# Two-layer feed-forward after gated retention on one core: the first four retention chunks in another order, and six tiles in the first run instead of five

## The chip, the cores and the metric

The kernel runs on one core of one Trainium2 chip. The metric is the device time of one execution, in microseconds (us). The kernel before was timed three times: 582.33, 582.37 and 582.92 us, median 582.37 us.

## The reference, cut to what matters

```python
# attention: retention with one decay per head, q, k, v are (2, 8, 768, 64)
gamma = 1.0 - 2.0 ** (-5.0 - np.arange(H))
scale = 1.0 / np.sqrt(D)
for t in range(S):
    state = gamma * state + einsum('bhd,bhe->bhde', k[:, :, t], v[:, :, t])
    y[:, :, t] = scale * einsum('bhd,bhde->bhe', q[:, :, t], state)
# y becomes x, (1536 tokens, 512); then two layers, w_in (512, 2048), w_out (2048, 512)
x = (mish(x @ w_in)) @ w_out          # h * tanh(log1p(exp(h)))
x = (elu(x @ w_in2)) @ w_out2
```

All of it is float32.

## The kernel before, in words

**Retention.** The 768 steps of each of the two batches are cut into six chunks of 128, twelve chunks in all, numbered so that chunks 0, 2, 4 ... are batch 0 and 1, 3, 5 ... batch 1. Each chunk has a tile `qk` (queries and keys, head dimension across partitions) and a tile `kv` (keys and values, time across partitions), 512 KB each. Chunks 0 to 3 use the functions `scores` (matmuls q·k into `sc`, L227, then the decay mask on VectorE, L234), `scale_k` and `scale_q` (GpSimd products `kd`, L188, and `qd`, L203, `qd` from chunk 2 on) and `attend` (y from state and `qd`, L251, y from v and masked scores, L257, and the new state `st`, L266; then `xh` on ScalarE, L275, `xl` on VectorE, L276, and the state on VectorE, L282 or L286). Chunks 4 to 11 use `scores64` (L309, L316; masks L324 and two states L331) and `attend64` (L353, L360; then copy `t` on ScalarE, L372, y + t on VectorE, L375, `xh`, L377, `xl`, L379). Four chunks make one block of 512 tokens, `x[0]`, `x[1]`, `x[2]`, each as a high and a low part.

**The layers.** The work is a list of tiles (layer, block, feature chunk f). Tile n does `up(n)` (12 matmuls into h: high weight by `xh`, low weight by `xh`, high weight by `xl`, L401), the activation, and three tiles later `down` (12 matmuls, L458). `runs` sets their order: layer 0, block 0, features 0 to FIRST-1; then block 1, features 0 to 7; then block 0, FIRST to 7; and so on. Only `x[0]` must stand before `up(0)`; `x[1]` must stand before tile FIRST. `steps` puts the retention steps of chunks 4 to 11 into the tiles' loop; in tile n they stand behind `up(n)` on TensorE.

**Weights.** They come as packed 64-bit words in 64 halves of 512 KB, `halves`, in the order of first use. Each half goes through `fetch` (DMA into `st`, four buffers, L109), `dec_fields` (two ScalarE activations, L116 and L118), `dec_join` (two VectorE instructions, L127 and L133; then the next `fetch`) and `dec_split` (high part `w0h` or `w1h` on ScalarE, L146, low part on GpSimd, L147). In tile n of the loop, `dec_split` is done for the halves that were joined in tile n-1, behind the retention's steps; at the end of the tile come `dec_join` for the halves whose fields were made in tile n-1, and `dec_fields` for one or two new halves, as `credit` and the due times `need` have it.

**Order.** Instructions are issued in the written order, each engine is a queue. All DMAs are issued by SyncE (SP), also in the written order. Half k of the weights is called half k below, its parts high k and low k.

Of the kernel before, what the change touches and what calls it, by code (L numbers as in the profile page):

```python
# [36 lines left out]
Q = P // 2  # L37
N_MASK, N_TQ, N_TK = H * P, NPAIR * P, CPB * H
N_CT = N_MASK + N_TQ + N_TK
FIRST = 5  # L40


@with_exitstack
def retention_then_two_ffn(
# [134 lines left out]
    def scale_k(c):  # L179
        kv = raw[c][1]  # L180
        i = c // B
        early = c < CPT

        rows = P if i < CPB - 1 else Q
        kd = (gpool if early else qd_p).tile(
            [P, H, D], F32, tag="gl" if early else "kd", name="kd"
        )
        nc.gpsimd.tensor_tensor(  # L188
            out=kd[:rows], in0=kv[:rows, 0], in1=tk[:rows, i].to_broadcast([rows, H, D]),
            op=ALU.mult,  # L190
        )
        scaled[c] = (None, kd)

    def scale_q(c):
        qk = raw[c][0]
        i = c // B
        early = c < CPT
        if i == 0:
            return
        qd = (gpool if early else qd_p).tile(  # L200
            [P, NPAIR, P], F32, tag="gh" if early else "qd", name="qd"
        )
        nc.gpsimd.tensor_tensor(out=qd, in0=qk[:, 0], in1=tabs.get(i, tq), op=ALU.mult)  # L203
        scaled[c] = (qd, scaled[c][1])

    def load_tab(i):
        tabs[i] = qd_p.tile([P, NPAIR, P], F32, tag="tab", name="tab", bufs=2)
# [5 lines left out]
    def scale_chunk(c):  # L213
        scale_k(c)
        scale_q(c)

    def psum(tag, name):
        return (psh if tag == "h" else psa).tile([P, NPAIR, P], F32, tag=tag, name=name)
# [17 lines left out]

        return rest

    def attend(c, tags=("h", "h")):

        kv = raw.pop(c)[1]
        at, (qd, kd) = scored.pop(c), scaled.pop(c)
        i = c // B
        v = kv[:, 1]
        state = states[c % B]
        y = psum(tags[0], "y")


        if i:
            for j in range(NPAIR):  # L250
                nc.tensor.matmul(  # L251
                    y[:, j], state[:, j], qd[:, j],
                    start=j == 0, stop=False, skip_group_check=True,
                )
        for j in range(NPAIR):
            for r in range(2):
                nc.tensor.matmul(  # L257
                    y[r * D:(r + 1) * D, j], v[:, 2 * j + r], at[:, r, j],
                    start=not i, stop=True, skip_group_check=True,
                )  # L260
        if i < CPB - 1:
            st = psum(tags[1], "st")
            for j in range(NPAIR):
                for r in range(2):
                    sl = slice(r * D, (r + 1) * D)
                    nc.tensor.matmul(  # L266
                        st[sl, j, sl], kd[:, 2 * j + r], v[:, 2 * j + r], start=True, stop=True
                    )

        def rest():  # L270
            b, o = divmod(c, CPT)
            if o == 0:
                x[b] = new_x(b)
            xh, xl = (a[:, :, o * P:(o + 1) * P] for a in x[b])
            nc.scalar.copy(out=xh, in_=y)  # L275
            nc.vector.tensor_tensor(out=xl, in0=y, in1=xh.bitcast(F32), op=ALU.subtract)  # L276
            if i < CPB - 1:
                for r in range(2):
                    sl = slice(r * D, (r + 1) * D)
                    if i:  # L280
                        new = compact[c % B] = slots[c % B][0]
                        nc.vector.tensor_tensor(  # L282
                            out=new[sl], in0=st[sl, :, sl], in1=state[sl, :, sl], op=ALU.add
                        )
                    else:
                        nc.vector.tensor_copy(state[sl, :, sl], st[sl, :, sl])  # L286

        return rest

# [200 lines left out]
    with tc.manual_schedule():  # L490
# [9 lines left out]
        for c, tag in ((2, "xh1"), (3, "xl1")):  # L500
# [6 lines left out]
                qk.rearrange("p a (j t) -> p a j t", t=P),  # L507
                kv.rearrange("p a (h d) -> p a h d", d=D),
            )
        for c in (2, 3):  # L510
            nc.sync.dma_start(
                out=raw[c][1].rearrange("p a h d -> p (a h d)"), in_=qkv[c, :, 2 * DM:]
            )
            fetch()
        fetch()
        fetch()
        started = done = 0
        N = len(tiles)
# [8 lines left out]
        def join():  # L527
            nonlocal started
            dec_fields(started)
            dec_join(started)  # L530
            started += 1

        def split_w():
            nonlocal done
            dec_split(done)
            done += 1

        ta, th, tb = ("a0", "a1"), ("h", "h"), ("a2", "a3")
        for i in range(3):
            warm = psa.tile([P, NPAIR, P], F32, tag=f"a{i}", name="warm")  # L540
            nc.tensor.matmul(warm, states[0][:, 0], states[0], start=True, stop=True)
        scale_chunk(0)
        scores(0, ta)()
        scale_chunk(1)
        scores(1, th)()
        scale_chunk(2)
        attend(0, tb)()
        scores(2, ta)()
# [12 lines left out]
        join()  # L561
        dec_fields(started)
        split_w()
        load_chunk(5)
        joined, credit = done, 0.0
        started += 1
# [14 lines left out]
        for n in range(N + LAG):  # L581
            todo = steps.get(n, [])
            rests = []
            if n < N:
                up(n)
                if todo:
                    f, *args = todo[0]
                    rests.append(f(*args))
            full = down(n - LAG) if n >= LAG else []
            for f, *args in todo[1:]:  # L590
                rests.append(f(*args))
            first_layer = n < N and tiles[n][0] == 0
            if first_layer:
                mish(n)
            elif n < N:
                elu_a(n)
            if 1 <= n <= N and tiles[n - 1][0] == 1:
                elu_b(n - 1)
            if full and not full[0][1]:
                for e in full:  # L600
                    evacuate(*e)
            for (f, c, *_), rest in zip(todo, rests):
                if f is scores64:
                    begun.add(c)
                    if c + 1 < NCH:
                        scale_k(c + 1)
                rest()
                if f is attend64 and c + 1 < NCH:
                    scale_q(c + 1)
                    if c % B and (c + 1) // B + 1 < CPB:  # L610
                        load_tab((c + 1) // B + 1)

            while next_load < NCH and scaled.get(next_load - 2, (None, 0))[0] is not None and (
                next_load - 2 in begun
            ):
                load_chunk(next_load)
                next_load += 1
            for k in range(done, joined):
                dec_split(k)
            done = joined  # L620
            if full and full[0][1]:
                for e in full:
                    evacuate(*e)
            if 1 <= n <= N and tiles[n - 1][0] == 1:
                split(n - 1)
            if any(f is attend64 and c == NCH - 1 for f, c, *_ in todo):
                actx.close()
                late["acc"] = ctx.enter_context(pool("acc12", 1))
                late["m"] = ctx.enter_context(pool("tmp2", 2))
                late["w"] = ctx.enter_context(pool("w2", EXTRA))  # L630
            if later:
                later.pop(0)()
            dec_join(*range(joined, started))
            joined = started
            ahead = range(started, min(started + 2 * GRP, NHALF))
            credit += max([1.0] + [
                (k - started + 1) / max(need[k] - n - 2, 0.5) for k in ahead
            ])
            credit = min(credit, 2.0)
            while credit >= 1 and room(started, n):  # L640
                dec_fields(started)
                started += 1
                credit -= 1
# [57 lines left out]
```

## Time and profile before

| | |
|---|---|
| median of three runs | 582.37 us |
| the profiled execution | 582.73 us, its span 580.8 us, 1.9 us around it |
| TensorE (PE) | 565.0 us busy, 97% of the span |
| VectorE (DVE), ScalarE (ACT), GpSimd (POOL) | 319.4, 283.0, 202.0 us busy |
| granted TensorE clock | full in all 40 slices (the higher level, 2.4 GHz) |
| DMA | 51.70 MB, 89 GB/s over the span; 0.9 busy in slices 3 and 4 |

The profile is one execution. Its views are the page, the waits of an engine (who waited for whom), the chain that ended last in order of time, the instructions of an engine in order of time, the busy time by stretch, and the DMA issues with their time to landing. Matmul records are hardware instructions: one float32 matmul of the program gives one or two.

### The profile page before, as it was taken

To read this page: it belongs to the slowest core of one execution; us is meant where nothing else is said; L and a number is where in the kernel's file an instruction comes from. 1 tells how busy PE (TensorE), PEld (TensorE's weight loads), DVE (VectorE), ACT (ScalarE), POOL (GpSimd) and SP (SyncE) were. 2 spreads that over 40 slices of the span, in tenths; PEclk is the share of its full clock that TensorE was granted. 3 is DMA by queue.
4 is the path that set the end of the run, shared out by engine and by line. 5 is a ranking of instruction groups with operands and counts; after the bars stand their busy time and mean duration, and the time that the engine had idled before them with its cause. 6 is when DMAs were issued, how large, how long until landed. Compare 5 with 4: busy or idle time off the path is not lost.

```text
span 580.8 us, 8785 instructions
## 1 busy us (share of the span) xinstructions
PE 565.0 (97%) x3510; PEld 464.7 (80%) x3510; DVE 319.4 (55%) x432; ACT 283.0 (49%) x508; POOL 202.0 (35%) x150
## 2 busy tenths in 40 slices
PE   6878999999999999999999999999999999999997
PEld 4766888888888888888888888888888888888885
DVE  3868555532665463212675995324788764524524
ACT  1575464345545642314656674435766653333331
POOL 1745343220222121110552695222564552222221
PEclk9999999999999999999999999999999999999999
DMA  8898642220333322000323232000333100100101
GB/s 318 336 311 260 208 150 76 75 72 1 120 99 108 102 80 73 0 1 0 119 99 110 72 109 72 1 0 2 109 110 108 37 0 2 72 1 0 74 0 72
DMA packets 15304, 51.70 MB, mean 89 GB/s; under 512 B 1696, under 2 KB 1696, under 8 KB 15264
## 3 DMA queue, kind: packets, MB, share of 16 engines
q1 hardware_dynamic: 15264, 51.15, 26.2%
q8 instruction: 27, 0.44, 0.3%
q14 instruction: 13, 0.11, 0.0%
HBM read 48.00 MB, written 3.15 MB: 88 GB/s over the span
## 4 chain that ended last, share of the span: by engine, by line
PE 91%; DMA 5%; POOL 2%; DVE 0%; issue 0%; SPq 0%; ACT 0%; POOLq 0%
PE a L458 45%; PE h L401 43%; DMA kv<-qkv 3%; DMA xl<-qkv 2%; PE y L353 1%; POOL kd L188 1%; POOL qd L203 1%; PE sc L309 1%; PE y L360 1%; DVE acc L471 0%; PE sc L316 0%; POOL w0l L147 0%; PE y L251 0%; PE y L257 0%; SPq L168 0%
## 5 line engine op out<-in xcount | busy, mean ns | idle before, releaser
L414 POOL TENSOR_TENSOR gl<-m,gh 128x512 fp32r<-128x512 f32 x48 | 69.6, 1449 | 106.0 <-ACT gh L413 106.0
L401 PE MATMUL h<-xh,w0h 128*128 128x512 f32 x384 | 103.3, 391 | 1.2 <-ACT w0h L146 1.0
L401 PE MATMUL h<-xh,w0l 128*128 128x512 f32 x384 | 102.8, 390 | 0.4 <-POOL w0l L147 0.4
L423 DVE TENSOR_TENSOR gl<-h,gh 128x512 fp32r<-128x512 f32 x48 | 33.2, 691 | 127.0 <-ACT h L422 123.8
L401 PE MATMUL h<-xl,w0h 128*128 128x512 f32 x384 | 102.6, 389 | 0.0
L431 ACT ACTIVATE e<-c 128x512 f32<-128x512 f32 x48 | 30.4, 632 | 123.3 <-DVE c L430 123.2
L430 DVE TENSOR_SCALAR c<-h 128x512 f32<-128x512 f32 x48 | 33.1, 690 | 101.7 <-PE h L401 101.7
L421 ACT ACTIVATE gh<-h 128x512 fp32r<-128x512 f32 x48 | 28.7, 597 | 120.5 <-PE h L401 120.5
L147 POOL TENSOR_TENSOR w0l<-f,w0h 128x512 fp32r<-128x512 f32 x32 | 42.4, 1327 | 124.3 <-ACT w0h L146 106.6
L401 PEld LDWEIGHTS h<-xh,w0l 128*128 128x128 f32 x384 | 72.0, 188 | 15.9 <-POOL w0l L147 0.8
L401 PEld LDWEIGHTS h<-xh,w0h 128*128 128x128 f32 x384 | 71.7, 188 | 16.3 <-ACT w0h L146 1.1
L401 PEld LDWEIGHTS h<-xl,w0h 128*128 128x128 f32 x384 | 72.1, 188 | 15.0
L458 PE MATMUL a<-gh,w1h 128*128 128x512 f32 x192 | 75.8, 395 | 0.0
L458 PE MATMUL a<-gl,w1h 128*128 128x512 f32 x192 | 74.8, 390 | 0.0
L458 PE MATMUL a<-gh,w1l 128*128 128x512 f32 x192 | 74.8, 390 | 0.0
L458 PE MATMUL a<-w1h,gh 128*128 128x512 f32 x192 | 74.7, 389 | 0.0
L458 PE MATMUL a<-w1l,gh 128*128 128x512 f32 x192 | 74.7, 389 | 0.0
L458 PE MATMUL a<-w1h,gl 128*128 128x512 f32 x192 | 74.7, 389 | 0.0
L133 DVE SCALAR_TENSOR_TENSOR f<-f,st 128x512 int32<-128x512 int32 x64 | 71.3, 1120 | 4.2
L147 POOL TENSOR_TENSOR w1l<-f,w1h 128x512 fp32r<-128x512 f32 x32 | 46.0, 1439 | 72.4 <-ACT w1h L146 51.0
L127 DVE SCALAR_TENSOR_TENSOR st<-st 128x512 int32<-128x512 int32 x64 | 68.7, 1080 | 0.5 <-ACT st L118 0.4
L116 ACT ACTIVATE f<-st 128x512 f32<-128x512 f32 x64 | 42.8, 669 | 4.3 <-DMA st<-w 4.2
(80 smaller groups left out, 688.9 us busy)
## 6 DMA issues: line engine op xcount, KB each, us to landing
st<-w SPq DMA_DIRECT2D x64, 512.0 KB, 3.8
qk<-qkv SPq DMA_DIRECT2D x10, 512.0 KB, 6.5
kv<-qkv SPq DMA_DIRECT2D x10, 512.0 KB, 7.4
out<-acc SPq DMA_DIRECT2D x12, 256.0 KB, 2.1
xh<-qkv SPq DMA_DIRECT2D x2, 512.0 KB, 9.5
xl<-qkv SPq DMA_DIRECT2D x2, 512.0 KB, 10.1
tab<-consts SPq DMA_DIRECT2D x4, 256.0 KB, 6.7
ct<-consts SPq DMA_DIRECT2D x1, 512.0 KB, 5.5
```

The source lines that it names most:

```text
L116: nc.scalar.activation(out=f, in_=t[:, :, 1].bitcast(F32), func=AF.Copy, scale=2.0 ** -112)
L127: nc.vector.scalar_tensor_tensor(out=t[:, :, 1], in0=t[:, :, 1], scalar=-(2 ** 31), in1=t[:, :, 0], op0=ALU.bitwise_and, op1=ALU.bitwise_or,)
L133: nc.vector.scalar_tensor_tensor(out=f, in0=f, scalar=3, in1=t[:, :, 1], op0=ALU.logical_shift_left, op1=ALU.bitwise_or,)
L147: nc.gpsimd.tensor_tensor(out=lo, in0=f, in1=hi.bitcast(F32), op=ALU.subtract)
L188: nc.gpsimd.tensor_tensor(out=kd[:rows], in0=kv[:rows, 0], in1=tk[:rows, i].to_broadcast([rows, H, D]), op=ALU.mult,)
L401: nc.tensor.matmul(h, u[:, k * P:(k + 1) * P], v[:, k], start=i == 0, stop=i == len(passes) - 1)
L414: nc.gpsimd.tensor_tensor(out=gl, in0=g, in1=gh.bitcast(F32), op=ALU.subtract)
L421: nc.scalar.activation(out=gh, in_=h, func=AF.Mish)
L423: nc.vector.tensor_tensor(out=gl, in0=h, in1=gh.bitcast(F32), op=ALU.subtract)
L430: nc.vector.tensor_scalar(out=c, in0=h, scalar1=0.0, scalar2=None, op0=ALU.min)
L431: nc.scalar.activation(out=e, in_=c, func=AF.Exp)
L458: nc.tensor.matmul(a, l, r, start=first and i == 0, stop=last and i == 2)
```

## The change

The first four chunks are written in another order, `attend` is split into `attend` (y) and `add_state` (the new state), and FIRST becomes 6. In the part ahead of the loop, three halves are joined as before, but two are split instead of three, and no further fields are made. The table for chunks 6 and 7 is loaded in tile 1 instead of ahead of the loop, chunk 5 earlier.

```diff
-FIRST = 5
+FIRST = 6
...
-        for c in (2, 3):
+        def load_early_kv(c):
             nc.sync.dma_start(
                 out=raw[c][1].rearrange("p a h d -> p (a h d)"), in_=qkv[c, :, 2 * DM:]
             )
-            fetch()
+
         fetch()
+        load_early_kv(2)
+        load_early_kv(3)
         fetch()
...
-        scale_chunk(0)
-        scores(0, ta)()
-        scale_chunk(1)
-        scores(1, th)()
-        scale_chunk(2)
-        attend(0, tb)()
-        scores(2, ta)()
-        load_chunk(4)
-        load_tab(2)
-        scale_chunk(3)
-        scores(3, th)()
-        join()
-        attend(1, th)()
-        split_w()
-        attend(2, tb)()
-        join()
-        attend(3, ta)()
-        split_w()
-        scale_chunk(CPT)
-        join()
-        dec_fields(started)
-        split_w()
-        load_chunk(5)
-        joined, credit = done, 0.0
-        started += 1
         for r in half:
             nc.scalar.copy(
                 out=mask64[r].rearrange("p r j t -> p (r j) t"),
                 in_=mask[r].rearrange("p r j t -> p (r j) t")[:, :, r],
             )
+        scale_k(0)
+        scores(0, ta)()
+        scale_k(1)
+        scores(1, th)()
+        for c, tags in ((0, tb), (1, th)):
+            rests = attend(c, tags[0]), add_state(c, tags[1])
+            for rest in rests:
+                rest()
+        load_chunk(4)
+        fetch()
+        load_chunk(5)
+        load_tab(2)
+        fetch()
+        scale_q(2)
+        scale_q(3)
+        scores(2, ta)()
+        scores(3, th)()
+        dec_fields(0)
+        dec_join(0)
+        scale_k(2)
+        scale_k(3)
+        rests = attend(2, tb[0]), attend(3, tb[1]), add_state(2, "h"), add_state(3, "h")
+        rests[0]()
+        dec_split(0)
+        rests[1]()
+        dec_fields(1)
+        dec_join(1)
+        scale_k(CPT)
+        dec_split(1)
+        rests[2]()
+        rests[3]()
+        dec_fields(2)
+        scale_q(CPT)
+        dec_join(2)
+        done, joined, started, credit = 2, 3, 3, 0.0
...
-        load_tab(3)
...
+            if n == 1:
+                load_tab(3)
```

Three places show how this moves instructions. The first is GpSimd ahead of the loop: `kd` and `qd` of chunks 2 and 3 (whose tiles are called xh and xl, numbers 115 and 117), then weights and chunk 4. Before:

```order
L188 TENSOR_TENSOR kd<-xh_115,ct 128x512
L203 TENSOR_TENSOR qd<-xh_115,ct 128x512
L188 TENSOR_TENSOR kd<-xl_117,ct 128x512
L203 TENSOR_TENSOR qd<-xl_117,ct 128x512
L147 TENSOR_TENSOR w0l<-f,w0h 128x512 x2
L188 TENSOR_TENSOR kd<-kv,ct 128x512
L203 TENSOR_TENSOR qd<-qk,tab 128x512
```

Now:

```order
L203 TENSOR_TENSOR qd<-xh_115,ct 128x512
L203 TENSOR_TENSOR qd<-xl_117,ct 128x512
L188 TENSOR_TENSOR kd<-xh_115,ct 128x512
L188 TENSOR_TENSOR kd<-xl_117,ct 128x512
L147 TENSOR_TENSOR w0l<-f,w0h 128x512
L188 TENSOR_TENSOR kd<-kv,ct 128x512
L147 TENSOR_TENSOR w0l<-f,w0h 128x512
```

The queries of chunks 2 and 3 are scaled ahead of their keys, and chunk 4's key product stands ahead of the low part of half 1.

The second is ScalarE in tiles 1 and 2, from chunk 4's copies `t` and `xh` on. Before:

```order
L372 COPY t<-y 64x256 x2
L377 CAST xh_507<-y 128x4x64 x2
L146 CAST w0h<-f 128x512
L116 ACTIVATE f<-st 128x512
L118 ACTIVATE st<-st 128x512
L116 ACTIVATE f<-st 128x512
L118 ACTIVATE st<-st 128x512
L421 ACTIVATE gh<-h 128x512
L422 ACTIVATE h<-h 128x512
L372 COPY t<-y 64x256 x2
L377 CAST xh_507<-y 128x4x64 x2
L146 CAST w1h<-f 128x512
```

Now:

```order
L368 COPY t<-y 64x256 x2
L373 CAST xh_501<-y 128x4x64 x2
L116 ACTIVATE f<-st 128x512
L118 ACTIVATE st<-st 128x512
L116 ACTIVATE f<-st 128x512
L118 ACTIVATE st<-st 128x512
L417 ACTIVATE gh<-h 128x512
L418 ACTIVATE h<-h 128x512
L368 COPY t<-y 64x256 x2
L373 CAST xh_501<-y 128x4x64 x2
L146 CAST w0h<-f 128x512
L146 CAST w1h<-f 128x512
```

High 3, the `w0h` that `up(3)` needs, stood behind chunk 4's `xh`; now it stands behind chunk 5's.

The third is VectorE in tiles 1 and 2, from `gl` of tile 1 to `gl` of tile 2: y + t and `xl` of chunk 4, masks and states of chunk 5, and the joins. Before:

```order
L423 TENSOR_TENSOR gl<-h,gh 128x512
L375 TENSOR_TENSOR y<-y,t 64x256 x2
L379 TENSOR_TENSOR xl_508<-y,xh_507 128x4x64 x2
L324 TENSOR_TENSOR at<-sc,mask_95 128x256 x2
L331 TENSOR_TENSOR state_97<-sc,compact_99 128x256
L331 TENSOR_TENSOR state_97<-sc,state_97 128x256
L127 SCALAR_TENSOR_TENSOR st<-st 128x512
L133 SCALAR_TENSOR_TENSOR f<-f,st 128x512
L423 TENSOR_TENSOR gl<-h,gh 128x512
```

Now:

```order
L419 TENSOR_TENSOR gl<-h,gh 128x512
L371 TENSOR_TENSOR y<-y,t 64x256 x2
L375 TENSOR_TENSOR xl_502<-y,xh_501 128x4x64 x2
L320 TENSOR_TENSOR at<-sc,mask_95 128x256 x2
L327 TENSOR_TENSOR state_97<-sc,compact_99 128x256
L327 TENSOR_TENSOR state_97<-sc,state_97 128x256
L127 SCALAR_TENSOR_TENSOR st<-st 128x512 x2
L133 SCALAR_TENSOR_TENSOR f<-f,st 128x512 x2
L419 TENSOR_TENSOR gl<-h,gh 128x512
```

The tile joins two halves where it joined one. By the same list, tiles 0 to 4 joined 1, 1, 2, 1 and 1 halves before; now they join 0, 2, 2, 2 and 1.

## Rows read from the trace of the kernel before

**Rows 1.** The page, busy time: engine, us, share of the span, instructions.

```profile
PE 565.0 (97%) x3510; PEld 464.7 (80%) x3510; DVE 319.4 (55%) x432; ACT 283.0 (49%) x508; POOL 202.0 (35%) x150
```

**Rows 2.** TensorE's waits, 20 us to the end: us in total, times, longest.

```profile
PE y L353 <- DVE state L331: 1.6, 1, 1.6
PE sc L316 <- POOL kd L188: 1.4, 1, 1.4
...
PE h L401 <- ACT w0h L146: 1.0, 1, 1.0
PE h L401 <- POOL w0l L147: 0.4, 1, 0.4
```

**Rows 3.** Busy time by stretch: us, then PE, PEld, DVE, ACT, POOL, clock, DMA share.

```profile
62.00:120.00 58.00, 58.00 (x683) 47.18 (x682) 31.33 (x54) 30.44 (x62) 19.68 (x15) 1.00 0.34 111
```

**Rows 4.** The chain that ended last, 0 to 120 us: start, us, what.

```profile
8.02 10.58 DMA xl<-qkv
...
18.67 1.50 POOL kd L188
20.18 1.25 POOL qd L203
...
61.47 2.72 PE h L401 x12
```

**Rows 5.** TensorE in order of time: start, us, line, out<-in, [idle before <- releaser].

```profile
24.34 1.19 PE L401 MATMUL h<-xh,w0h 128*128 128x512 f32 x4 [0.22 <-ACT xh L275]
...
33.03 0.24 PE L353 MATMUL y<-qd,state 64*64 64x64 f32 x1 [1.63 <-DVE state L331]
...
40.17 0.27 PE L353 MATMUL y<-qd,state 64*64 64x64 f32 x1
...
42.65 1.19 PE L401 MATMUL h<-xh,w0h 128*128 128x512 f32 x4
...
53.24 1.19 PE L401 MATMUL h<-xh,w0h 128*128 128x512 f32 x4 [0.95 <-ACT w0h L146]
54.83 1.21 PE L401 MATMUL h<-xh,w0l 128*128 128x512 f32 x4 [0.40 <-POOL w0l L147]
```

**Rows 6.** VectorE in order of time, the same columns.

```profile
26.77 1.42 DVE L133 SCALAR_TENSOR_TENSOR f<-f,st 128x512 int32<-128x512 int32 x1
...
33.98 0.69 DVE L133 SCALAR_TENSOR_TENSOR f<-f,st 128x512 int32<-128x512 int32 x1
...
38.61 0.42 DVE L331 TENSOR_TENSOR state<-sc,state 128x256 f32<-128x256 f32 x1
...
42.68 0.88 DVE L375 TENSOR_TENSOR y<-y,t 64x256 f32<-64x256 f32 x2 [0.59 <-ACT t L372]
...
46.12 2.05 DVE L127 SCALAR_TENSOR_TENSOR st<-st 128x512 int32<-128x512 int32 x2
48.10 2.38 DVE L133 SCALAR_TENSOR_TENSOR f<-f,st 128x512 int32<-128x512 int32 x2
...
51.10 0.88 DVE L375 TENSOR_TENSOR y<-y,t 64x256 f32<-64x256 f32 x2
```

**Rows 7.** ScalarE in order of time: high 3 and high 5.

```profile
36.90 0.64 ACT L146 CAST w0h<-f 128x512 fp32r<-128x512 f32 x1
...
52.55 0.63 ACT L146 CAST w0h<-f 128x512 fp32r<-128x512 f32 x1
```

**Rows 8.** GpSimd in order of time.

```profile
27.60 1.73 POOL L203 TENSOR_TENSOR qd<-qk,tab 128x512 f32<-128x512 f32 x1
...
45.75 1.27 POOL L147 TENSOR_TENSOR w1l<-f,w1h 128x512 fp32r<-128x512 f32 x1
47.67 1.66 POOL L203 TENSOR_TENSOR qd<-qk,tab 128x512 f32<-128x512 f32 x1 [0.64 <-POOL w1l L147]
52.47 1.04 POOL L188 TENSOR_TENSOR kd<-kv,ct 128x512 f32<-128x512 f32 x1 [3.15 <-PE sc L316]
```

**Rows 9.** DMA issues at 15.34 us: out<-in, KB, us to landing.

```profile
tab<-consts SPq DMA_DIRECT2D x1, 256.0 KB, 10.4
```

More of the change, by code (lines that the diff above doesn't have):

```diff
@@ L191, in scale_k @@
         )
-        scaled[c] = (None, kd)
+        scaled[c] = (scaled.get(c, (None,))[0], kd)
     def scale_q(c):
@@ L203, in scale_q @@
         nc.gpsimd.tensor_tensor(out=qd, in0=qk[:, 0], in1=tabs.get(i, tq), op=ALU.mult)
-        scaled[c] = (qd, scaled[c][1])
+        scaled[c] = (qd, scaled.get(c, (None, None))[1])
     def load_tab(i):
@@ L211, in load_tab @@
         )
-    def scale_chunk(c):
-        scale_k(c)
-        scale_q(c)
     def psum(tag, name):
@@ L237, in scores, with attend @@
         return rest
[L239 to L249, printed above, removed]
+    def attend(c, tag):
+        at, qd, v = scored.pop(c), scaled[c][0], raw[c][1][:, 1]
+        y = psum(tag, "y")
+        if c >= B:
             for j in range(NPAIR):
                 nc.tensor.matmul(
-                    y[:, j], state[:, j], qd[:, j],
+                    y[:, j], states[c % B][:, j], qd[:, j],
                     start=j == 0, stop=False, skip_group_check=True,
@@ L255, in attend @@
         for j in range(NPAIR):
-            for r in range(2):
+            for r, sl in enumerate(half):
                 nc.tensor.matmul(
-                    y[r * D:(r + 1) * D, j], v[:, 2 * j + r], at[:, r, j],
-                    start=not i, stop=True, skip_group_check=True,
-                )
[L261 to L268, printed above, removed]
+                    y[sl, j], v[:, 2 * j + r], at[:, r, j],
+                    start=c < B, stop=True, skip_group_check=True,
+                )
@@ L270, in rest @@
         def rest():
[L271 to L274, printed above, removed]
+            if c == 0:
+                x[0] = new_x(0)
+            xh, xl = (a[:, :, c * P:(c + 1) * P] for a in x[0])
             nc.scalar.copy(out=xh, in_=y)
             nc.vector.tensor_tensor(out=xl, in0=y, in1=xh.bitcast(F32), op=ALU.subtract)
[L277 to L286, printed above, removed]
+        return rest
@@ new lines, in add_state, with rest @@
+    def add_state(c, tag):
+        v, kd = raw.pop(c)[1][:, 1], scaled.pop(c)[1]
+        st = psum(tag, "st")
+        for j in range(NPAIR):
+            for r, sl in enumerate(half):
+                nc.tensor.matmul(
+                    st[sl, j, sl], kd[:, 2 * j + r], v[:, 2 * j + r], start=True, stop=True
+                )
+        def rest():
+            state = states[c % B]
+            for sl in half:
+                if c >= B:
+                    new = compact[c % B] = slots[c % B][0]
+                    nc.vector.tensor_tensor(
+                        out=new[sl], in0=st[sl, :, sl], in1=state[sl, :, sl], op=ALU.add
+                    )
+                else:
+                    nc.vector.tensor_copy(state[sl, :, sl], st[sl, :, sl])
@@ L525, in room @@
             return old < 0 or last_use[old] + LAG * i <= now
-        def join():
-            nonlocal started
-            dec_fields(started)
-            dec_join(started)
-            started += 1
[L533 to L536, printed above, removed]
         ta, th, tb = ("a0", "a1"), ("h", "h"), ("a2", "a3")
@@ L541, in retention_then_two_ffn @@
             nc.tensor.matmul(warm, states[0][:, 0], states[0], start=True, stop=True)
-        scale_chunk(0)
-        scores(0, ta)()
-        scale_chunk(1)
-        scores(1, th)()
-        scale_chunk(2)
-        attend(0, tb)()
-        scores(2, ta)()
-        load_chunk(4)
-        load_tab(2)
-        scale_chunk(3)
-        scores(3, th)()
-        join()
-        attend(1, th)()
-        split_w()
-        attend(2, tb)()
-        join()
-        attend(3, ta)()
-        split_w()
-        scale_chunk(CPT)
-        join()
-        dec_fields(started)
-        split_w()
-        load_chunk(5)
-        joined, credit = done, 0.0
-        started += 1
         for r in half:
```

## The prediction, made before the changed kernel ran

> **What bounds the kernel now.** I read the page first: TensorE is busy for 97% of the span [rows 1]. Then the busy time by stretch: from 62 us to 120 us TensorE is busy for 58.00 of 58.00 us [rows 3], and its list of waits has nothing after 62 us. So whatever the change does must show before about 62 us, as time in which TensorE waits, and from there on it is carried to the end one for one. The chain that ended last says how that first part hangs together: chunk 3's values land at 8.02 + 10.58 = 18.6 us, GpSimd makes `kd` and `qd` of chunk 3 from them one after the other, and only then come that chunk's y, its `xh` and `up(0)` [rows 4], which begins at 24.34 us [rows 5]. Behind it TensorE waits four times: 1.6 us for a state, 1.4 us for `kd` of chunk 5, and 1.0 us and 0.4 us for the weights of `up(4)` [rows 2]. About 0.7 us more lie in pieces of 0.3 us and less. A perfect reorder could win the head start of `up(0)` plus these, no more.
>
> I compare one point: the start of `up(5)`, 61.47 us in the chain [rows 4]. Both programs give TensorE the same matmuls up to there (`up` 0 to 4, chunks 4 to 7, two `down`), and the same in sum behind it.
>
> **Part 1, the start of `up(0)`.** `qd` of chunk 3 now stands ahead of both `kd`. The SP queue still issues chunk 3's values as its eleventh transfer (the weight half only changes places with chunk 2's values), so they still land at 18.6 us. Then `kd` of chunk 3 ends at 18.67 + 1.50 = 20.2 us [rows 4], while y and `xh` of chunk 3 are made beside it; behind `kd` only the eight small state matmuls (0.6 us) stand ahead of `up(0)`. I get 21.0 us against 24.34, a head start of 3.3 us. The mask copies that moved to the front lie in ScalarE's first idle time and cost nothing.
>
> **Part 2, chunk 4's y (L353).** It began at 33.03 us, released by a state [rows 5]. Now VectorE has, ahead of that state, a whole join of half 1, four state sums and the join of half 2; and `qd` of chunk 4 needs its table, which is the 18th transfer and not the 17th. It landed at 15.34 + 10.4 = 25.7 us [rows 9]; five and a half transfers of 512 KB lay between 18.6 and 25.7 us, 1.3 us each, so now 27.0 us. That gives 28.9 us at the least (table, `qd` of 1.3 to 1.7 us, issue). At the most, the join's second instruction waits for that `qd`: the two met before, and took 1.42 and 1.73 us [rows 6, 8] where such instructions take 0.69 and about 1.3 us apart. Then the join ends at 27.0 + 1.3 + 0.7 = 29.0, and `gl`, mask and state (0.6, 0.7, 0.4) end at 30.7 us. I take 30.3 us, near the upper end, since both stand ready at the same moment. The lead has shrunk to 2.7 us. The 1.4 us for `kd` of chunk 5 are saved, as chunk 5 is now loaded ahead of tile 0, but the next step takes that back.
>
> **Part 3, `up(3)`: the step that decides.** Before, high 3 was made at 36.90 us [rows 7], a tile early, and `up(3)` began at 42.65 us with no wait [rows 5]. Now high 3 is queued on ScalarE behind `xh` of chunk 5. Ahead of that `xh` is y + t on VectorE, and ahead of y + t are now two joins. So `up(3)` hangs on this chain: chunk 4's y to the end of chunk 5's states, 33.03 to 38.61 + 0.34 = 5.9 us [rows 5, 6]; the joins, J; `gl`, 0.6 us; y + t to `up`, 51.10 to 53.24 = 2.15 us [rows 5, 6], a stretch that holds `xh` and the high half at 52.55 [rows 7].
>
> J: four instructions of 0.69 us [rows 6] make 2.8 us alone. The one round with two joins in this trace took from 46.12 to 48.10 + 2.38 = 50.48, which is 4.4 us [rows 6], with two GpSimd products, of 1.27 and 1.66 us, in the same time [rows 8]. In the new order `qd` of chunk 6 and `kd` of chunk 7 come ready in this round; if each holds up a join for its whole length (1.3 and 1.0 us), J = 5.1 us. I take that, because `qd` comes free as soon as chunk 5's y is done, in the middle of the joins.
>
> `up(3)` begins at 30.3 + 5.9 + 5.1 + 0.6 + 2.15 = 44.05 us, 1.4 us later than before. Its second third waits for low 3, which GpSimd makes in 1.3 us behind high 3 while the first four matmuls take 1.0: 0.3 us more.
>
> **Part 4, from `up(3)` to `up(5)`.** Before it took 61.47 - 42.65 = 18.8 us. TensorE's own need is 18.3 us (0.5 us of small gaps out): low 5 is still made behind `kd` of chunk 8, which waits for chunk 7's matmuls [rows 8], so the 0.95 + 0.40 us at `up(4)` stay in another form. But VectorE now has two joins in each of these rounds too. A round from y + t to y + t took 51.10 - 42.68 = 8.4 us with J = 4.4 [rows 6], so it is J + 4.0. In these rounds two low parts and a `qd` stand on GpSimd; with two whole products and a remainder in the way I take J = 5.5, a round of 9.55 us, two of them 19.1 us: now longer than TensorE's need. `up(5)`, which before needed no new weight, now takes high 7 and low 7 from this chain, 0.6 us more for low 7.
>
> **Sum.** 44.05 + 0.3 + 19.1 + 0.6 = 64.05 us against 61.47 (each rounded): 2.6 us later. The profiled execution took 582.73 us, so 585.3 us; the median of the runs is 0.36 us under it, so 585.0 us. Edits at nothing: the moved mask copies, and the table of chunk 6, loaded later (its `qd` waits for chunk 5's y anyway).
>
> **A rule beside the row.** What the rows show is that a join of 0.69 us can take 1.42 us beside a GpSimd product [rows 6, 8]. The Trainium skill (SBUF — State Buffer, Who interferes with whom) says why that may be: a VectorE instruction with two inputs in SBUF and a GpSimd instruction share a port pair, and whoever comes first holds it for the whole instruction. The trace agrees as far as this one meeting shows. The rule speaks against the change, and taken to its end it is the last rival below.
>
> **Rivals.**
> *The joins meet nothing, faster, 0.16.* If GpSimd's products fall outside the joins and chunk 4's y starts at its lower bound, `up(3)` begins at 28.9 + 5.9 + 2.8 + 2.75 = 40.35, and `up(5)` 18.3 us plus 0.3 later, at 58.95: 2.5 us earlier, 579.9 us. For it: the join's instruction at 33.98 us took 0.69 us with nothing in its way [rows 6]. Against it: GpSimd now has two low parts, a `kd` and a `qd` in each tile, 4.9 us of work that becomes ready right then. It decides at J of about 3.7 us.
> *It comes out even, 0.22.* With J = 4.4 as in the one round shown, TensorE's own 18.3 us decide after `up(3)`: 30.3 + 5.9 + 4.4 + 2.75 + 0.3 + 18.3 = 61.95, 0.5 us later, 582.9 us by the median. The head start and the new waits cancel.
> *Forecast, 0.50:* J of 5 to 6 us, 1.2 to 4.4 us later by the same sum.
> *Three products in every round, 0.12.* J = 2.8 + 3 x 1.3 = 6.7 us, rounds of 10.7 us: 30.3 + 5.9 + 6.7 + 2.75 + 0.3 + 21.4 + 0.6 = 67.95, 6.5 us later, 588.9 us. This is what the rule of the Trainium skill on the shared pair (SBUF — State Buffer, Who interferes with whom) would give if GpSimd always came first; one round in the trace had two.
> That the change does not do what it says (no head start) would need chunk 3's values to land later; nothing in the SP order does that, so it has no share of its own.
>
> **How the numbers follow.** Around 0.2% (1.2 us) is what a measurement of this kernel can tell from no change: 581.2 to 583.5 us. Faster is the first rival, 0.16; the same is the even case, 0.22; slower is the forecast and the last rival, 0.62. The range for 8 in 10 leaves about a tenth out on either side: 581.0 us (inside the faster case) to 587.6 us (between forecast and last rival). The forecast's own range is 583.6 to 586.8 us.
>
> **What would show it.** In the new profile `up(0)` should begin near 21 us; chunk 4's y near 30; `up(3)` should begin near 44 us, released by `w0h` on ScalarE after an idle time of some 4 us; the rounds with two joins should take over 5 us from L127 to L133's end; `up(5)` should wait for weights near 63 us. The forecast is wrong if `up(3)` begins before 42.65 us, if the two-join rounds take about 3 us, or if TensorE waits anywhere after 70 us.

## The result, and the profile after

The changed kernel takes 586.23 us (median; 585.48 to 586.83, 4 runs) beside 582.35 us for the kernel before on the same chip (581.85 to 582.92, 4 runs). The ratio is 1.0066, 95% interval 1.0048 to 1.0084: slower by 0.66%, 3.9 us. The forecast was 585.0 us, 2.6 us slower. The profiled execution took 585.66 us with a span of 583.6 us, 2.8 us more than the span before.

The page of the changed kernel (`up` is now L397, `down` L454, the later y L349, the states L327, y + t L371, `gl` L419; the lines up to 203 have kept their numbers) has TensorE at 97% still. New is in the line `PEclk`, which gives the granted clock in tenths, one digit for each fortieth of the span: 9 in every slice before, it is 7 and 8 in the third and fourth.

```profile
PE 568.9 (97%) x3510; PEld 466.8 (80%) x3510; DVE 319.2 (55%) x432; ACT 283.8 (49%) x508; POOL 200.7 (34%) x150
...
PEclk9978999999999999999999999999999999999999
```

TensorE's waits from 20 to 75 us (total, times, longest) answer to [rows 2]; after 75 us there are none.

```profile
PE h L397 <- ACT w0h L146: 3.0, 1, 3.0
PE y L349 <- DVE state L327: 2.0, 1, 2.0
PE h L397 <- POOL w0l L147: 1.9, 2, 1.4
PE y L349 <- POOL qd L203: 0.6, 1, 0.6
```

TensorE in order of time, for [rows 5]: `up(0)`, chunk 4's y, chunk 5's y, `up(3)` (its first and last third), `up(4)`, and the second and last third of `up(5)`.

```profile
21.38 1.19 PE L397 MATMUL h<-xh,w0h 128*128 128x512 f32 x4
...
29.01 0.26 PE L349 MATMUL y<-qd,state 64*64 64x64 f32 x1 [0.58 <-POOL qd L203]
...
36.57 0.24 PE L349 MATMUL y<-qd,state 64*64 64x64 f32 x1 [2.04 <-DVE state L327]
...
43.12 2.07 PE L397 MATMUL h<-xh,w0h 128*128 128x512 f32 x4 [3.00 <-ACT w0h L146]
46.70 1.70 PE L397 MATMUL h<-xl,w0h 128*128 128x512 f32 x4
...
53.95 1.19 PE L397 MATMUL h<-xh,w0h 128*128 128x512 f32 x4
56.54 1.20 PE L397 MATMUL h<-xh,w0l 128*128 128x512 f32 x4 [1.39 <-POOL w0l L147]
...
64.91 1.20 PE L397 MATMUL h<-xh,w0l 128*128 128x512 f32 x4 [0.55 <-POOL w0l L147]
65.95 1.08 PE L397 MATMUL h<-xl,w0h 128*128 128x512 f32 x4
```

The head start of `up(0)` is there: 21.38 against 24.34 us, 3.0 us. By chunk 5's y it is 3.6 us (36.57 against 40.17, [rows 5]). All of it is gone at `up(3)`, which waits 3.0 us for high 3 and starts 0.5 us later than before. `up(5)` ends at 65.95 + 1.08 = 67.03 us; before it ended at 61.47 + 2.72 = 64.19 [rows 4]. That is 2.84 us, the whole difference of the spans, so nothing more is lost later.

Busy time by stretch (PE, PEld, DVE, ACT, POOL, clock, DMA share, GB/s) shows a second thing that [rows 3] had no sign of: from 38 to 48 us TensorE had a granted clock of 0.50, its 1.2 GHz level.

```profile
34.00:38.00 4.00, 1.96 (x65) 1.56 (x66) 3.47 (x10) 3.79 (x8) 1.19 (x2) 0.97 0.91 344
38.00:48.00 10.00, 7.00 (x90) 5.72 (x83) 9.50 (x16) 5.02 (x11) 4.80 (x4) 0.50 0.71 232
48.00:49.00 1.00, 1.00 (x24) 0.67 (x24) 0.04 (x1) 0.56 (x2) 0.00 (x0) 0.98 0.65 197
```

The same stretch of the kernel before, in the same view:

```profile
38.00:48.00 10.00, 9.47 (x215) 7.76 (x213) 7.82 (x16) 6.87 (x15) 6.14 (x6) 1.00 0.91 303
```

The last third of `up(3)` in the kernel before:

```profile
44.60 1.07 PE L401 MATMUL h<-xl,w0h 128*128 128x512 f32 x4
```

At the lower clock `up(3)` takes 46.70 + 1.70 - 43.12 = 5.28 us, where before it took 44.60 + 1.07 - 42.65 = 3.02 us. It looks like nearly the whole loss, and it is not: from the end of `up(3)` to `up(4)` the changed kernel needs 53.95 - 48.40 = 5.55 us, the kernel before 53.24 - 45.67 = 7.57 us, mostly because before it idled there (it was busy for 6.10 of the 7.57 us; now it is busy throughout). The account runs: +0.47 us at the start of `up(3)`, +2.26 by the slow clock, -2.02 behind `up(3)`, +1.00 as low 5 is waited for 1.39 us in place of 0.40, and the rest, 1.1 us, from there to the end of `up(5)`: half of it is the new wait for low 7 (0.55 us), the other half lies in pieces of 0.3 us and less.

VectorE in order of time, for [rows 6], shows the three rounds with two joins (L127 x2, L133 x2) and the y + t that they hold up.

```profile
32.59 0.69 DVE L419 TENSOR_TENSOR gl<-h,gh 128x512 fp32r<-128x512 f32 x1 [3.27 <-ACT h L418]
33.30 0.88 DVE L371 TENSOR_TENSOR y<-y,t 64x256 f32<-64x256 f32 x2
...
36.80 1.28 DVE L127 SCALAR_TENSOR_TENSOR st<-st 128x512 int32<-128x512 int32 x2
38.00 2.38 DVE L133 SCALAR_TENSOR_TENSOR f<-f,st 128x512 int32<-128x512 int32 x2
...
40.99 0.88 DVE L371 TENSOR_TENSOR y<-y,t 64x256 f32<-64x256 f32 x2
...
44.43 2.40 DVE L127 SCALAR_TENSOR_TENSOR st<-st 128x512 int32<-128x512 int32 x2
46.75 1.28 DVE L133 SCALAR_TENSOR_TENSOR f<-f,st 128x512 int32<-128x512 int32 x2
49.55 0.69 DVE L419 TENSOR_TENSOR gl<-h,gh 128x512 fp32r<-128x512 f32 x1 [1.52 <-ACT h L418]
50.78 0.88 DVE L371 TENSOR_TENSOR y<-y,t 64x256 f32<-64x256 f32 x2 [0.54 <-ACT t L368]
...
54.06 0.75 DVE L320 TENSOR_TENSOR at<-sc,mask 128x256 f32<-128x256 f32 x2 [1.20 <-PE sc L312]
...
55.52 3.22 DVE L127 SCALAR_TENSOR_TENSOR st<-st 128x512 int32<-128x512 int32 x2
58.66 1.28 DVE L133 SCALAR_TENSOR_TENSOR f<-f,st 128x512 int32<-128x512 int32 x2
...
61.03 0.88 DVE L371 TENSOR_TENSOR y<-y,t 64x256 f32<-64x256 f32 x2 [0.49 <-ACT t L368]
```

GpSimd, for [rows 8], shows the products that fall into these rounds: one into the first, one into the second, two into the third.

```profile
37.85 1.37 POOL L203 TENSOR_TENSOR qd<-qk,tab 128x512 f32<-128x512 f32 x1 [0.94 <-PE y L349]
...
44.39 1.29 POOL L147 TENSOR_TENSOR w1l<-f,w1h 128x512 fp32r<-128x512 f32 x1
...
55.22 1.27 POOL L147 TENSOR_TENSOR w0l<-f,w0h 128x512 fp32r<-128x512 f32 x1
56.44 1.75 POOL L147 TENSOR_TENSOR w1l<-f,w1h 128x512 fp32r<-128x512 f32 x1
```

The rounds take 38.00 + 2.38 - 36.80 = 3.58, 46.75 + 1.28 - 44.43 = 3.60 and 58.66 + 1.28 - 55.52 = 4.42 us. Apart, their four instructions would take 2.8 us, so each product costs its round some 0.8 us, less than its own length.

ScalarE, for [rows 7]: the fields of half 3 (28.91) and half 4 (30.25), `mish(1)` behind them, and high 3 at 42.44 us, which before was made at 36.90.

```profile
28.91 0.68 ACT L116 ACTIVATE f<-st 128x512 f32<-128x512 f32 x1 [1.10 <-DMA st<-w]
...
30.25 0.69 ACT L116 ACTIVATE f<-st 128x512 f32<-128x512 f32 x1
...
31.43 0.57 ACT L417 ACTIVATE gh<-h 128x512 fp32r<-128x512 f32 x1
...
42.44 0.63 ACT L146 CAST w0h<-f 128x512 fp32r<-128x512 f32 x1
```

`up(1)` had ended at 28.4 us (its last third in TensorE's order of time is below), but `mish(1)` stands in ScalarE's queue behind the fields of two halves, and the first of them waits 1.10 us for half 3 to land. In the kernel before, half 4's fields alone stood between `mish(0)` and `mish(1)`; those of half 3 were made ahead of the loop, at 25.84 us, without a wait. The wait is new because the change issues half 3's transfer only at 19.30 us, behind chunk 4, chunk 5 and their table; before, it was one of three transfers issued from 9.52 to 11.84 us, ahead of these. So `mish(1)` starts at 31.43 us, and `gl`, y + t, `xh` and the states of chunk 5's y follow from it. Most of the 2.04 us for which TensorE waits there come from this: experiment 3 leaves 0.72 us of them.

```profile
27.36 1.07 PE L397 MATMUL h<-xl,w0h 128*128 128x512 f32 x4
```

### The profile page after: what moved, and what is told of

Same layout as the page of the kernel before. It is cut to its first block, busy times and chain, and to the rows that moved or that the text cites. A ratio compares the mean times of both kernels' runs of the same rounds, so it can differ in the third digit from the quotient of the medians.

```text
span 583.6 us, 8781 instructions
## 1 busy us (share of the span) xinstructions
PE 568.9 (97%) x3510; PEld 466.8 (80%) x3510; DVE 319.2 (55%) x432; ACT 283.8 (49%) x508; POOL 200.7 (34%) x150
## 4 chain that ended last, share of the span: by engine, by line
PE 89%; DVE 1%; POOL 0%; ACT 0%; issue 0%; POOLq 0%
PE a L454 44%; PE h L397 43%; PE y L349 1%; DVE acc L467 0%; PE y L356 0%; PE sc L305 0%; PE sc L312 0%; POOL w0l L147 0%; DVE y L371 0%; DVE xl L375 0%; ACT t L368 0%; ACT xh L373 0%; POOLq L147 0%
## 5 line engine op out<-in xcount | busy, mean ns | idle before, releaser
L397 PE MATMUL h<-xh,w0h 128*128 128x512 f32 x384 | 104.3, 394 | 3.0 <-ACT w0h L146 3.0
L397 PE MATMUL h<-xh,w0l 128*128 128x512 f32 x384 | 103.8, 392 | 1.9 <-POOL w0l L147 1.9
L419 DVE TENSOR_TENSOR gl<-h,gh 128x512 fp32r<-128x512 f32 x48 | 33.2, 691 | 129.3 <-ACT h L418 125.4
L397 PE MATMUL h<-xl,w0h 128*128 128x512 f32 x384 | 103.3, 391 | 0.0
L397 PEld LDWEIGHTS h<-xh,w0h 128*128 128x128 f32 x384 | 72.1, 189 | 18.5 <-ACT w0h L146 3.6
L397 PEld LDWEIGHTS h<-xh,w0l 128*128 128x128 f32 x384 | 72.5, 189 | 18.0 <-POOL w0l L147 2.8
L397 PEld LDWEIGHTS h<-xl,w0h 128*128 128x128 f32 x384 | 72.6, 189 | 15.3
L454 PE MATMUL a<-gh,w1h 128*128 128x512 f32 x192 | 75.8, 395 | 0.0
L454 PE MATMUL a<-gh,w1l 128*128 128x512 f32 x192 | 74.8, 390 | 0.0
L454 PE MATMUL a<-gl,w1h 128*128 128x512 f32 x192 | 74.8, 390 | 0.0
L454 PE MATMUL a<-w1h,gh 128*128 128x512 f32 x192 | 74.7, 389 | 0.0
L454 PE MATMUL a<-w1l,gh 128*128 128x512 f32 x192 | 74.7, 389 | 0.0
L454 PE MATMUL a<-w1h,gl 128*128 128x512 f32 x192 | 74.7, 389 | 0.0
L127 DVE SCALAR_TENSOR_TENSOR st<-st 128x512 int32<-128x512 int32 x64 | 71.3, 1123 | 0.8 <-ACT st L118 0.8
L133 DVE SCALAR_TENSOR_TENSOR f<-f,st 128x512 int32<-128x512 int32 x64 | 68.5, 1079 | 3.8
```

Source lines behind the costliest of these rows:

```text
L127: nc.vector.scalar_tensor_tensor(out=t[:, :, 1], in0=t[:, :, 1], scalar=-(2 ** 31), in1=t[:, :, 0], op0=ALU.bitwise_and, op1=ALU.bitwise_or,)
L133: nc.vector.scalar_tensor_tensor(out=f, in0=f, scalar=3, in1=t[:, :, 1], op0=ALU.logical_shift_left, op1=ALU.bitwise_or,)
L397: nc.tensor.matmul(h, u[:, k * P:(k + 1) * P], v[:, k], start=i == 0, stop=i == len(passes) - 1)
L419: nc.vector.tensor_tensor(out=gl, in0=h, in1=gh.bitcast(F32), op=ALU.subtract)
L454: nc.tensor.matmul(a, l, r, start=first and i == 0, stop=last and i == 2)
```

## The experiments

**The theory** after the result: the weights' lead in front of tile 0 was cut by one weight half, so high 3 hangs on the first round with two joins and on all that is queued ahead of it; this makes `up(3)` late, and the later weights follow. **The rivals**: the fall of the clock is a cost of its own; the sixth tile costs; the new order of chunks 0 to 3 costs by itself.

**1. Fill TensorE's idle time behind `up(2)`.** Eight matmuls are added that nobody reads.

```
                 up(n)
+                if n == 2:
+                    fill(n, 8)
```

> The changed kernel with eight extra matmuls (result unread) behind up(2), in the idle time ahead of chunk 5's y. Theory A (the 2.04 us of idle time ahead of chunk 5's y cost TensorE its clock, and the 10.2 us at the lower level stretched up(3) from 3.0 to 5.7 us): the granted clock stays 1.00 from 30 to 50 us, up(3) begins as before near 43 us but takes 3.0 to 3.3 us, and the time falls by 2.0 to 2.6 us, to 583.6 to 584.2 us. Rival B (the clock fell for another reason, such as the many small matmuls): the stretch at 0.5 stays, the time is 586 us. Rival C (the queue on VectorE decides up(4) and up(5) whatever up(3) takes): clock 1.00, but less than 1 us won.

Measured: 586.49 us, ratio 1.0067 (1.0055 to 1.0079). No gain: the time is the one of rival B, though the clock is not. The stretch at half clock became shorter (0.72 as a mean of 44 to 50 us, 1.00 before that), but `up(3)` waited 5.7 us and began at 44.86 us. The reason stands on VectorE and GpSimd in this execution, VectorE first:

```profile
36.86 2.13 DVE L127 SCALAR_TENSOR_TENSOR st<-st 128x512 int32<-128x512 int32 x2
38.92 3.20 DVE L133 SCALAR_TENSOR_TENSOR f<-f,st 128x512 int32<-128x512 int32 x2
```

```profile
37.13 1.31 POOL L188 TENSOR_TENSOR kd<-kv,ct 128x512 f32<-128x512 f32 x1 [4.63 <-DMA kv<-qkv]
38.41 1.70 POOL L203 TENSOR_TENSOR qd<-qk,tab 128x512 f32<-128x512 f32 x1
40.30 1.26 POOL L188 TENSOR_TENSOR kd<-kv,ct 128x512 f32<-128x512 f32 x1 [0.19 <-DMA kv<-qkv]
```

The round took 38.92 + 3.20 - 36.86 = 5.26 us in place of 3.58, with three GpSimd products beside it. Why chunk 6's values landed over 1 us later here than in the changed kernel, where its `kd` ran at 35.87 us ahead of the round, is open; the fills need not be the reason, since experiment 4, with the same instructions in tiles 0 to 2 and no fills, has this `kd` at 37.69 us and a round of 4.40 us. The Trainium skill describes such a meeting (SBUF — State Buffer, Who interferes with whom): a VectorE instruction with two inputs in SBUF contends with a GpSimd instruction that reads SBUF. The trace agrees that they hold each other up, as the joins' four instructions, 2.8 us alone, needed 5.3; it is again some 0.8 us for each product, where these products themselves took 1.3 to 1.7 us. So this run is no clean test of the clock: the round grew while the clock stayed up longer.

**2. High 3 ahead of the round.** Half 3 is split at the head of tile 2, ahead of chunk 5's y + t, and its join ends before half 4's begins.

```
+            if n == 2:
+                dec_split(done)
+                done += 1
             for (f, c, *_), rest in zip(todo, rests):
...
-            dec_join(*range(joined, started))
+            if n == 1:
+                for k in range(joined, started):
+                    dec_join(k)
+            else:
+                dec_join(*range(joined, started))
```

> The changed kernel with high 3 and low 3 made in tile 2 ahead of chunk 5's copies, and half 3 joined whole ahead of half 4. Theory A (high 3 behind chunk 5's xh made the 3.0 us wait of up(3)): up(3) begins near 40.1 us with under 0.3 us of wait. The clock still falls near 38 us, as the idle time ahead of chunk 5's y stays, so up(3) still takes 5 to 6 us; 2 to 3 us won, 583.3 to 584.3 us. Rival C (the joins on VectorE decide): up(3) is early, but up(4) still begins near 54 us, less than 1 us won.

Measured: 581.95 us, ratio 0.9991 (0.9982 to 0.9999), 4.3 us less than the changed kernel. TensorE in order of time: `up(3)` without a wait, chunk 6's y, and the second third of `up(5)`.

```profile
40.19 1.19 PE L397 MATMUL h<-xh,w0h 128*128 128x512 f32 x4
...
45.58 0.24 PE L349 MATMUL y<-qd,compact 64*64 64x64 f32 x1 [2.20 <-DVE compact L327]
...
62.18 1.20 PE L397 MATMUL h<-xh,w0l 128*128 128x512 f32 x4 [0.55 <-POOL w0l L147]
```

`up(3)` is 2.9 us earlier. The gain is larger than the 2 to 3 us expected, and the fall of the clock near 38 us, expected to stay, is gone: the clock is 1.00 from 16 us on. What is late next is chunk 6's state, since y + t of chunk 5 still stands behind both joins.

**3. The fields of half 4 behind chunk 4's `xh`.** They move out of `mish(1)`'s way, to the end of tile 1.

```
             if n == 1:
+                dec_fields(4)
                 load_tab(3)
...
-                dec_fields(started)
+                if n or started < 4:
+                    dec_fields(started)
```

> The changed kernel with the fields of half 4 made in tile 1 behind chunk 4's xh, not in tile 0 ahead of mish of tile 1, where ScalarE waits for its DMA. Theory A: mish of tile 1 comes 1.1 us earlier, chunk 5's y begins near 35.4 us and the idle time ahead of it is 0.9 us and not 2.04; 1 us won by that alone (585.2 us), and 3 to 3.5 us (582.7 to 583.2 us) if the shorter gap also leaves the clock at 1.00. Rival B: the clock falls in the same place all the same, 585.2 us.

Measured: 585.19 us, ratio 1.0050 (1.0035 to 1.0065), 1.0 us less than the changed kernel, though the two intervals overlap. In the profiled execution, the fastest of six (583.66 us), `mish(1)` begins at 29.88 us and chunk 5's y at 35.08 us, 1.5 us earlier each; `up(3)` still waits 2.54 us, until 41.38 us. The clock still falls: it is 0.86 as a mean of 38 to 50 us.

**4. Five tiles.** `FIRST = 5`, all else as changed.

> The changed kernel with FIRST = 5, all else as changed. Tiles 0 to 2 are the same instructions, so theory A expects the same 2.0 us and 3.0 us waits, the same stretch at the lower clock, and only the waits of up(5) for high 7 and low 7 gone: 585.3 to 586 us. Rival D (the sixth tile's extra weight halves are what costs): back at 582.4 us or under.

Measured: 585.45 us, ratio 1.0048 (1.0036 to 1.0060), 0.8 us less, again with overlapping intervals. `up(5)` no longer waits for weights, `up(3)` still does: 4.2 us, until 43.99 us.

**5. The kernel before with the shorter lead.** Chunks, loads and `FIRST` stay; the fields of half 3 and the split of half 2 leave the part ahead of the loop.

```
         join()
-        dec_fields(started)
-        split_w()
         load_chunk(5)
-        joined, credit = done, 0.0
-        started += 1
+        joined, credit = started, 0.0
```

> The kernel before with nothing of the chunks' order changed, only the weights' lead cut as in the change: the fields of half 3 and the split of half 2 are left out ahead of the loop, so that half 3 is joined in a round of two joins in tile 1 and its high part comes behind chunk 5's xh. Chunks 0 to 3, the values' loads and FIRST stay as before. Theory A (the late high part of half 3 makes up(3) wait, and the idle TensorE loses its clock): up(3), at 42.65 us before, waits over 2 us more for high 3, the granted clock falls to 0.5 for a stretch around 38 to 50 us, and the time is 584.5 to 588 us. Theory B (the new order of chunks 0 to 3 and of the loads is what costs): the cut alone does little, the clock stays at 1.00, 582 to 583.3 us.

Measured: 585.83 us, ratio 1.0056 (1.0043 to 1.0069). This edit alone, without anything of the new order, costs 3.4 us. `up(3)` on TensorE, and the busy time by stretch:

```profile
45.02 1.71 PE L401 MATMUL h<-xh,w0h 128*128 128x512 f32 x4 [2.26 <-ACT w0h L146]
```

```profile
44.00:50.00 6.00, 4.88 (x18) 3.17 (x20) 5.76 (x10) 2.83 (x7) 3.98 (x3) 0.72 0.97 337
```

It is the changed kernel's picture in the old order: the wait for high 3, and behind the idle time the fall of the clock.

**6. The kernel before with six tiles.** `FIRST = 6` and nothing else.

> The kernel before with FIRST = 6 and nothing else. Theory A (the sixth tile matters only through rounds of two joins that come earlier): joins go 1, 1, 2, 2 in tiles 0 to 3, up(3) has its weights as early as before, a later tile may wait up to 1 us: 582.3 to 583.6 us. Theory C (the sixth tile itself costs, wherever the weights are): 584 us or more.

Measured: 583.64 us, ratio 1.0021 (1.0012 to 1.0030): 1.2 us, a hair above the 582.3 to 583.6 us of theory A and below the 584 us of theory C. The clock is 1.00 throughout; `up(5)` waits 0.55 us for low 7, as in the changed kernel. The sixth tile is a small part of the loss.

**7. Edits 2 and 3 together.**

> The changed kernel with both of the edits that gained time: half 3 split in tile 2's head and joined whole ahead of half 4, and the fields of half 4 made in tile 1 behind chunk 4's xh. Theory A (two separate waits, up(3) for high 3 and chunk 5's y for the state of chunk 1): the gains add in part, up(3) near 39.5 us without a wait, clock full from 20 us on, 580.3 to 581.6 us. Theory B (one chain; what is taken out of tile 1 comes back in tile 2 or 3 as a wait for chunk 6's state): 581.7 to 582.5 us, as with the first edit alone.

Measured: 581.27 us, ratio 0.9975 (0.9964 to 0.9985), as theory A expected. The two gains seem to add in part; the interval just touches that of experiment 2.

**8. Edits 2, 3 and 4 together.**

> The same with FIRST = 5, so that only one round ahead of tile 5 has two joins. Theory A: the wait for a state in a round with two joins goes from tile 3 on, and up(5) does not wait for its weights: 579.8 to 581.2 us. Theory B (the sixth tile's join only moves, as its half has to be joined later beside later tiles): within 0.3 us of the kernel with FIRST = 6.

Measured: 579.33 us, ratio 0.9949 (0.9935 to 0.9962). This is a little less than the 579.8 us expected at the least; it beats the kernel before by 3.1 us and the changed one by 6.9. Its waits on TensorE from 20 us on are seven of 1.0 us and less. Two of them, and the stretch from 62 us on, in which TensorE has no idle time:

```profile
PE h L397 <- ACT w0h L146: 1.0, 1, 1.0
PE y L349 <- DVE state L327: 0.7, 1, 0.7
```

```profile
62.00:120.00 58.00, 58.00 (x624) 47.28 (x623) 31.73 (x56) 29.56 (x60) 18.34 (x14) 1.00 0.34 107
```

**9. The new order with the old lead.** `FIRST = 5`, and the two steps of experiment 5 are put back ahead of the loop.

```
         dec_join(2)
-        done, joined, started, credit = 2, 3, 3, 0.0
+        dec_fields(3)
+        dec_split(2)
+        done, joined, started, credit = 3, 3, 4, 0.0
```

> The changed kernel with FIRST = 5 and with the weights' lead of the kernel before: the fields of half 3 and the split of half 2 come ahead of the loop again, so that only the order of chunks 0 to 3 and of the loads stays changed. Theory A (the lead alone decides; the new order by itself gains what up(0) gains): high 3 is split in tile 1 as in the kernel before, up(3) does not wait for it, the clock stays at 1.00 from 20 us on, up(0) is at 22 to 23.5 us, and the time is 579.8 to 581.8 us. Theory B (the new order costs by itself, through the late values and states): 582.5 us or more.

Measured: 583.37 us, ratio 1.0008 (0.9999 to 1.0017). It is better than experiment 4 (1.0048), from which it differs by the lead alone, but the expected 579.8 to 581.8 us was missed, and the number is that of theory B, by which the new order costs by itself. ScalarE shows how: the fields of half 3 wait for their transfer, and high 2 and `mish(0)` wait behind them.

```profile
29.00 0.66 ACT L116 ACTIVATE f<-st 128x512 f32<-128x512 f32 x1 [3.23 <-DMA st<-w]
...
30.10 0.60 ACT L146 CAST w0h<-f 128x512 fp32r<-128x512 f32 x1
30.60 0.59 ACT L417 ACTIVATE gh<-h 128x512 fp32r<-128x512 f32 x1
```

TensorE's list of waits gives the price, paid at chunk 4's y:

```profile
PE y L349 <- DVE state L327: 5.1, 1, 5.1
```

So in the new order the lead can't stand where it stood: its data are not there yet. Half 3's transfer is issued at 19.40 us here, behind chunk 4, chunk 5 and their table, and lands at 29.0; it is the changed order of the loads that makes it late. The clock falls here too (0.65 as a mean of 30 to 38 us).

**10. Two fills.** Six unread matmuls behind `up(2)`, nine ahead of `up(3)`.

```
+                if n == 3:
+                    fill(2, 9)
                 up(n)
+                if n == 2:
+                    fill(n, 6)
```

> The changed kernel with 6 matmuls that nobody reads behind up(2) and 9 more ahead of up(3), some 1.5 and 2.3 us of TensorE at full clock in its two idle stretches. Theory A (the fall of the clock is a cost of its own): the clock stays at 1.00 through up(3), its 12 matmuls take 3.0 us in place of 5.2, chunk 6's y starts near 46.5 us in place of 48.79, and the time is 583.4 to 584.6 us. Theory B (the wait for the weights is the cost and the slow stretch only fills it): up(3) starts no earlier than 43 us, the time won at full clock comes back as waits for low 5 ahead of up(5), and the time is 585.2 to 586.5 us.

Measured: 586.01 us, ratio 1.0058 (1.0039 to 1.0078), so theory B's number. The profiled execution was the slowest, with the long round of experiment 1, `up(3)` at 45.41 us and a slow clock again. But each execution comes with its mean granted clock over the span, and here they differ:

```
two fills: 584.75 (clock 0.999) 585.52 (0.999) 585.97 (1.000) 586.06 (0.997) 587.53 (0.997) 588.43 (0.994)
```

In the three with the clock at 0.999 and over, the kernel is still 2.0 to 3.2 us above the 582.80 us of the kernel before. No trace of these three was kept, so what they waited for, and whether the fills themselves cost something in them, is not shown. Experiment 5 has one such execution without fills: at a clock of 0.999 it took 584.76 us, 2.3 us above the 582.42 us of the kernel before.

## Why the prediction was right, and where it was wrong

The sign was right, and so was the mechanism that decides. High 3 stands behind the first round with two joins, and `up(3)` waits for it. From there to `up(5)` the forecast had the chain of weights as what paces the work; it does so only in part, with the waits for low 5 and low 7 (1.9 us), and for the rest TensorE is busy, first at half clock. Experiment 5 shows that this cut of the lead is enough, experiment 2 that the loss goes when high 3 leaves the round. The size was 3.9 us in place of 2.6; within the profiled executions, where the sum was made, 2.84 us. That the sum came so close is partly luck, as its parts show.

**Part 1** held: `up(0)` at 21.38 us for 21.0 forecast, with two terms off that nearly cancelled. `kd` of chunk 3 waited for the values until 19.35 us, not 18.6, and then took 1.04 us, not 1.50.

**Part 2** took 30.3 us for chunk 4's y, near the upper bound; it came at 29.01 us, at the lower one. The join did not meet `qd` of chunk 4, which began at 27.67 us, behind it.

**Part 3** gave 44.05 us for `up(3)`; it was 43.12 us, from terms that were off both ways. *Chunk 4's y to the end of chunk 5's states* was carried over from before as 5.9 us; it took 36.80 - 29.01 = 7.8 us. This is the step that missed a mechanism: the change puts the fields of two halves, 3 and 4, between `mish(0)` and `mish(1)` on ScalarE where half 4's alone stood, and makes half 3 land later. I had priced every move on VectorE and GpSimd but not on this queue, nor asked when half 3 lands. With half 4's fields out of the way, in experiment 3, the same step took 35.30 - 28.86 = 6.4 us; in experiment 9, where high 2 and `mish(0)` stand behind the wait for half 3, TensorE idles for 5.1 us. *J* was 3.58 us in place of 5.1. `kd` of chunk 7 came at the round's end (40.26 us), and `qd` of chunk 6, which ran into it, held it up by 0.8 us, not by its whole length as the sum had it.

With 3.6 us for J the sum as it stood would have put `up(3)` at 42.55 us, ahead of the 42.65 us at which the prediction itself was to be wrong, and `up(5)`, by the even case's working, at 61.15 us, 0.3 us earlier than before. So the time came out in the forecast's range because ScalarE's queue and the clock added what the joins did not; that is luck, and the sign that the rounds take over 5 us failed (3.58, 3.60 and 4.42 us). J of 5.1 us was a possible value all the same: experiment 4 had 4.40 us and experiment 1, with three products in the round, 5.26. Which products fall into a round depends on when values land, and so J is a range, 3.6 to 5.3 us in these executions, and not a number.

**Part 4** gave rounds of 9.55 us with a J of 5.5. From y + t to y + t they took 50.78 - 40.99 = 9.8 and 61.03 - 50.78 = 10.25 us, so their length was right, and what filled them was not: the joins took 3.6 us in the first and 4.4 in the second. Much of the rest came from TensorE. In the first round `gl` waits 1.52 us for `mish(3)`, since `up(3)` ran at half clock; in the second the masks wait 1.20 us for chunk 7's matmuls. The sum assumed the full clock throughout; that assumption failed. `up(5)` was put at 64.05 us with the wait for low 7 in it, and so its end at 66.77 us; it ended at 67.03.

**What the clock is worth.** As the only cost, a fall of the clock does not fit: the execution of experiment 5 at a clock of 0.999 still lost 2.3 us. But clock and time go together. In experiment 5 the two executions with a mean clock of 0.994 took 586.54 and 586.65 us, some 2 us more than the one at 0.999. In experiment 3 the three at 0.997 took 583.66 to 584.61 us, the three at 0.994 took 585.77 to 586.74. Whether the lower clock makes these executions longer, or a longer wait makes both, is not shown: no trace has the changed kernel's long wait with the clock at 1.00 throughout, and in the profiled executions of both fill experiments the wait grew and the clock fell all the same. Slow matmuls and waits can stand in for each other here, as the 2.02 us behind `up(3)` show. So of the 3.9 us some 2 to 3 remain with the clock nearly full, by one execution of experiment 5 and three of experiment 10, and the rest, 1 to 2 us, goes with the clock.

**The rivals.** That the joins meet nothing was nearly so (3.6 us, the point at which it was to decide was 3.7), yet the gain did not come, for the two reasons above: the ScalarE queue and the clock. That three products meet every round did not happen in the changed kernel. In experiment 1 three products met one round, and even then J was 5.26 us and not this rival's 6.7.

## What to carry to other kernels

Where work that is prepared ahead (here the split of the weights) rides in the same in-order queues as the work that it feeds, starting the main work earlier only pays if the preparation starts earlier as well; otherwise the head start is waited off at the first step that needs what was prepared late. When a step is moved on a queue, ask of every engine what now stands behind it and whether its data have landed: a step that waits for a transfer stalls everything queued behind it, whoever that is for. And before blaming a slow stretch, compare also what follows it: time lost there may be idle time that the other kernel spends a little later.

## What the runs showed of the hardware that was not expected

TensorE's granted clock fell to 0.50, the 1.2 GHz level, from 38 to 48 us in the changed kernel, after it had idled 2.04 us and while it went on to idle 3.00 us more. The kernel before idled 1.63 and 1.45 us in the same part [rows 2] and kept 1.00. The Trainium skill (TensorE: Matmul & The Clock Gate, Part 1: The HAM clock gate) names these two levels and ties them to how busy the array has been; the trace agrees so far.

The same program can have the fall or not. Beside experiments 9 and 10, three of 17 executions of the kernel before had a mean clock of 0.994, and they took 584.23, 584.29 and 584.93 us; those at 0.998 and over took 582.18 to 583.20. The three lie 1.5 to 2.2 us above the middle of the others. Beside experiments 1 to 8 it was one of 36 (584.14 us). The mean over the span does not say where the clock fell: in the profiled execution of experiment 2 (mean 0.996) it was between 8 and 16 us, ahead of `up(0)`. Nor need a fall cost anything: in that experiment the four executions at 0.997 took 581.12 to 581.96 us and the three at 1.000 took 581.82 to 582.50, though two at 0.996 took 583.01 and 583.42.

On VectorE, a GpSimd product beside the joins cost them some 0.8 us: 3.58 and 3.60 us for a round with one product, 4.42 us with two and 5.26 us with three, against 2.8 us for the four instructions apart.
